# One pool of 2 KB pages, 120 f pairs by seven products, and rounded copies fetched by GpSimd transfers

## The chip, the cores and the metric

The kernel runs on one core of one Trainium2 chip. The metric is the device time of one execution in microseconds (us); the median of three runs stands for the kernel. The engines are TensorE (PE, with PEld for its weight loads), VectorE (DVE), ScalarE (ACT), GpSimd (POOL) and SyncE (SP), which issues the transfers. SBUF is the on-chip memory, PSUM the eight banks that TensorE writes into.

## The reference

Two steps, cut to what matters. The inputs are float32, 4 batches of 6080 tokens with 256 channels; the hidden width f is 2048; w_in and w_out arrive in a 64-bit type.

```python
def _attn_ref(q, k, v, tau):                       # 4 x 6080 x 256 each
    qn = q / (np.linalg.norm(q, axis=1, keepdims=True) + 1e-06)
    kn = k / (np.linalg.norm(k, axis=1, keepdims=True) + 1e-06)
    s = kn.transpose(0, 2, 1) @ qn / tau           # 256 x 256 for each batch, the gram
    a = softmax(s)                                 # over the last axis
    return v @ a
def _moe_ref(x, w_in, w_out):                      # x: 24320 x 256
    h = x @ w_in                                   # 256 -> 2048
    g = np.where(h >= 1, h, np.where(h <= -1, 0.0, (h + 1) ** 2 / 4.0))
    return (g @ w_out).astype(np.float32)          # 2048 -> 256
```

## The kernel before

**What is computed where.** For each batch b, `gram_chunk` and `softmax` make the attention matrix, and `make_W7` (or `make_W` in the first batch) multiplies it into w_in, so that h = v @ (a @ w_in) is one product. The tokens of a batch are cut into six blocks k: five of 2 x 512 tokens and a last one of 2 x 480 (`pairs`). The hidden width is cut into eight pieces i of 256 ("f pairs", two halves of 128). One group is one (b, k, i); there are 4 x 6 x 8 = 192. `h_ops` makes the h of a group as a 2 x 2 block product in seven instead of eight block products (`strassen`); `sat_ops`, `square_ops` and `max_ops` apply the activation; `operand` makes from each of the four blocks the operand of the second product.

**Three matmuls for one product.** The matmuls take the float32r type. To keep precision, every operand is split into a high part (a copy rounded to float32r: a cast on ACT, or on DVE) and a low part (source minus high part: a subtraction on DVE, or on POOL). `mm3` (line 594) issues high x high, high x low and low x high. So one block product is three matmuls of 128 x 128 weights by 512 or 480 columns.

**The second product.** `o_ops` multiplies the four blocks of a group with w_out into four PSUM banks O00, O01, O10, O11, summed over i. Written directly that is eight block products (24 matmuls) for a group. For the first `SPLIT[b][k]` values of i, `strassen_o` does seven instead: four direct ones, and three in a chain into bank O01, on sums of the blocks. These cost other work: `combos` makes three sums of the activations in four subtractions (POOL or DVE); the sums have to be split into high and low parts in turn; and when the last i of them is done, the banks are copied or added out into SBUF between the three stages of the chain (`copy` on ACT and line 1071 on DVE). The summed weights lie in `wsum`; those of the fourth i are parked in DRAM and fetched again for each batch (`guest`). The table SPLIT adds up to 80 of the 192 groups.

**Gram and value copies.** `gram_chunk` loads 256 tokens of k and q (512 KB, on the SP queue), rounds them on ACT (line 603, 54 times), subtracts on DVE (line 604) and has 12 matmuls of 256 columns on PE. `make_V` loads the values of a block, makes four differences of them (line 879, POOL or DVE) and splits seven operands into high (line 885 on ACT or 887 on DVE) and low (line 889 on DVE).

**What sets the order.** The kernel is a list of operations, each with an engine (some with a second one in `other`), its reads and writes, and a due time. `Order.run` goes through them with a table of costs and picks for each engine the next one; what comes out is the fixed instruction order of every engine. Due times come from the tables DUES and LATE. Buffers come from pools of one size and one purpose each (`g`, `u`, `c`, `q`, `m5`, `h22`, `kqs`); who gets a free one is decided in the same run. Each engine works through its own queue strictly in order, so a late instruction holds everything behind it. `tie` makes a POOL operation wait for a given DVE operation, so that both don't use SBUF at once.

## Time and profile before

| what | value |
|---|---|
| median of 3 runs | 2113.44 us (2112.09 to 2113.67) |
| span of the profiled execution | 2112.1 us |
| PE busy | 2102.0 us, 9634 records |
| DVE busy | 1925.6 us, 91% of the span |
| ACT busy | 1786.5 us, 85% |
| POOL busy | 665.0 us, 31% |
| DMA | 374 MB, mean 177 GB/s |

The profiled execution's own time is its span, 2112.1 us, which is the lower end of the three runs and 1.3 us under their median. The granted TensorE clock is 1.000 for the whole span. A busy share counts the time from an instruction's start to its end, where instructions of one engine may overlap; the pitch (from one start to the next) is shorter than the duration. For PE the ends are modelled, so its busy share says little, and the pitch of its matmuls is the better measure.

### The profile page before, as it was taken

How to read it: one execution, taken by the hardware profiler on the slowest of the kernel's cores; microseconds unless marked ns; L12 is line 12 of the kernel's file. 1: busy time of each engine (PE TensorE's matmuls, PEld its weight loads, DVE VectorE, ACT ScalarE, POOL GpSimd, SP SyncE). 2: the span in 40 equal slices, each digit the busy share in tenths (PEclk: the TensorE clock that was granted, in tenths of full speed). 3: DMA queues.
4: the chain of work that ended last, by engine and by line, in shares of the span. 5: the costliest groups of instructions: out<-in, count | busy, mean ns of one | idle time of the engine just before them, and what ended most of it. 6: DMA issues, size and time to landing. Idle time of an engine off the chain costs nothing.

```text
span 2112.1 us, 29105 instructions
## 1 busy us (share of the span) xinstructions
PE 2102.0 (100%) x9634; PEld 1752.6 (83%) x9634; DVE 1925.6 (91%) x3024; ACT 1786.5 (85%) x3255; POOL 665.0 (31%) x621
## 2 busy tenths in 40 slices
PE   9999999999999999999999999999999999999999
PEld 7878888788888888888888888888888888888887
DVE  8998898989899999999889899999997989989987
ACT  6698898988898888889889888888888878888886
POOL 0133133333232333314323233332332333342331
PEclk9999999999999999999999999999999999999999
DMA  9854466544756535544475555454456442432431
GB/s 385 310 204 168 153 230 205 170 162 146 253 173 221 193 139 186 181 163 155 161 243 199 188 185 181 152 197 158 146 196 212 154 145 90 142 127 93 139 112 68
DMA packets 124568, 374.16 MB, mean 177 GB/s; under 512 B 17280, under 2 KB 48896, under 8 KB 121856
## 3 DMA queue, kind: packets, MB, share of 16 engines
q1 hardware_dynamic: 124416, 372.29, 50.4%
q8 instruction: 76, 1.25, 0.2%
q14 instruction: 76, 0.62, 0.1%
HBM read 300.94 MB, written 71.31 MB: 176 GB/s over the span
## 4 chain that ended last, share of the span: by engine, by line
PE 93%; DVE 2%; DMA 2%; ACT 1%; issue 0%; SPq 0%; POOL 0%; ACTq 0%; DVEq 0%; POOLq 0%
PE bank L594 93%; DMA kq<-kq 1%; DMA raw_mem<-w_out 1%; PE bank L1141 1%; DVE u_mem L943 0%; DMA raw_mem<-kq 0%; DVE x L963 0%; DVE u_mem L488 0%; DVE u_mem L491 0%; ACT u_mem L938 0%; DVE w_mem L836 0%; ACT y_mem L1156 0%; ACT u_mem L934 0%; DVE x L1064 0%; DVE u_mem L486 0%
## 5 line engine op out<-in xcount | busy, mean ns | idle before, releaser
L594 PE MATMUL bank<-v,w_mem 128*128 128x512 f32 (+1 forms) x3216 | 832.6, 389 | 2.3 <-ACT bank L774 1.0
L594 PEld LDWEIGHTS bank<-v,w_mem 128*128 128x128 f32 x3216 | 598.8, 188 | 129.0 <-DVE bank L777 4.2
L594 PE MATMUL bank<-x,wout 128*128 128x512 f32 (+1 forms) x2670 | 681.0, 388 | 0.0
L594 PEld LDWEIGHTS bank<-x,wout 128*128 128x128 f32 x2670 | 500.0, 188 | 100.1 <-POOL x L963 0.5
L934 ACT ACTIVATE u_mem<-bank 128x512 f32<-128x512 f32 (+1 forms) x576 | 339.7, 593 | 168.9 <-PE bank L594 163.0
L938 ACT ACTIVATE u_mem<-u_mem 128x512 f32<-128x512 f32 (+1 forms) x768 | 471.6, 628 | 6.6
L943 DVE TENSOR_TENSOR u_mem<-bank,u_mem 128x512 f32<-128x512 f32 (+1 forms) x576 | 385.5, 676 | 70.5 <-ACT u_mem L938 68.9
L963 POOL TENSOR_TENSOR x<-u_mem,x 128x512 fp32r<-128x512 f32 (+1 forms) x162 | 210.0, 1299 | 421.5 <-DVE x L960 104.9
L963 DVE TENSOR_TENSOR x<-u_mem,x 128x512 fp32r<-128x512 f32 (+1 forms) x410 | 308.9, 767 | 3.4 <-ACT x L958 2.6
L958 ACT CAST x<-u_mem 128x512 fp32r<-128x512 f32 (+1 forms) x414 | 247.6, 615 | 34.8 <-DVE u_mem L943 20.9
L594 PE MATMUL bank<-g,wout 128*128 128x512 f32 (+1 forms) x882 | 232.8, 388 | 0.0
L594 PE MATMUL bank<-x,w_mem 128*128 128x512 f32 (+1 forms) x816 | 224.2, 389 | 0.3 <-DVE u_mem L943 0.3
L594 PEld LDWEIGHTS bank<-g,wout 128*128 128x128 f32 x882 | 165.2, 188 | 33.4 <-POOL g L963 0.4
L943 DVE TENSOR_TENSOR u_mem<-mh_mem,u_mem 128x512 f32<-128x512 f32 (+1 forms) x192 | 147.9, 770 | 37.2 <-ACT u_mem L938 36.9
L594 PEld LDWEIGHTS bank<-x,w_mem 128*128 128x128 f32 x816 | 151.9, 188 | 32.6 <-DVE u_mem L943 1.1
L1005 POOL TENSOR_TENSOR q<-u_mem 128x512 f32<-128x512 f32 (+1 forms) x81 | 104.2, 1286 | 193.9 <-DVE u_mem L943 66.6
L934 ACT ACTIVATE u_mem<-mh_mem 128x512 f32<-128x512 f32 (+1 forms) x192 | 120.0, 625 | 27.0 <-DVE mh_mem L781 24.9
L777 DVE TENSOR_TENSOR bank<-bank,mh_mem 128x512 f32<-128x512 f32 (+1 forms) x198 | 135.5, 684 | 5.5 <-PE bank L594 3.4
L781 DVE TENSOR_TENSOR mh_mem<-bank,mh_mem 128x512 f32<-128x512 f32 (+1 forms) x198 | 133.6, 675 | 1.5 <-PE bank L594 0.8
L594 PE MATMUL bank<-x,wsum 128*128 128x512 f32 (+1 forms) x492 | 131.6, 388 | 0.2 <-DVE c L1071 0.2
L879 POOL TENSOR_TENSOR raw_mem<-raw_mem 128x512 f32<-128x512 f32 (+1 forms) x56 | 71.9, 1284 | 166.8 <-DVE x L963 63.6
L963 POOL TENSOR_TENSOR g<-u_mem,g 128x512 fp32r<-128x512 f32 (+1 forms) x55 | 72.2, 1314 | 165.1 <-DVE g L960 38.8
(143 smaller groups left out, 2689.8 us busy)
## 6 DMA issues: line engine op xcount, KB each, us to landing
w_mem<-w_d SPq DMA_DIRECT2D x160, 896.0 KB, 4.6
raw_mem<-kqT SPq DMA_DIRECT2D x60, 512.0 KB, 5.4
w_d<-w_mem SPq DMA_DIRECT2D x32, 896.0 KB, 4.2
raw_mem<-kq SPq DMA_DIRECT2D x51, 512.0 KB, 5.5
kq<-kq SPq DMA_DIRECT2D x20, 1024.0 KB, 9.7
raw_mem<-vT SPq DMA_DIRECT2D x40, 512.0 KB, 6.2
q<-wop_d SPq DMA_DIRECT2D x30, 512.0 KB, 5.7
outT<-c SPq DMA_DIRECT2D x51, 256.0 KB, 2.1
```

The lines of the kernel that those rows point to most:

```text
L594: nc.tensor.matmul(out, lhsT=lhs(a), rhs=rhs(c), start=start and m == 0, stop=stop and m == 2, skip_group_check=skip)
L777: op("DVE", dve_us(n), lambda: nc.vector.tensor_tensor(out=bb.ap[:, :n], in0=z.ap[:, :n], in1=m5.ap[:, :n], op=ALU.add), r=[z, m5], w=[bb] ...
L781: op("DVE", dve_us(n), lambda: nc.vector.tensor_tensor(out=h22.ap[:, :n], in0=z.ap[:, :n], in1=m5.ap[:, :n], op=ALU.add), r=[z, m5], w=[h2 ...
L879: return lambda: e.tensor_tensor(out=part(o), in0=part(a), in1=part(c), op=ALU.subtract)
L934: op("ACT", act_us(n), lambda: nc.scalar.activation(half_of(u, x, n), h.ap[:, :n], IDENTITY_SAT240, scale=240.0), r=[h], w=[u.parts[x]], t ...
L938: op("ACT", act_us(n * (1 + (x is None))), lambda: nc.scalar.activation(part_of(u, x, n), part_of(u, x, n), AF.Square, bias=0.5, scale=1.0 ...
L943: op("DVE", dve_us(n), lambda: nc.vector.tensor_tensor(out=us(), in0=h.ap[:, :n], in1=us(), op=ALU.max), r=[h], w=[u.parts[x]], h=[u], due ...
L958: op("ACT", act_us(cols), lambda x=x: nc.scalar.copy(part(0, x), part_of(u, x, n)), r=of(u.parts, x), w=of(t.parts, x), h=[u, t], due=due, ...
L963: return lambda: e.tensor_tensor(out=part(1, x), in0=part_of(u, x, n), in1=f32(part(0, x)), op=ALU.subtract)
L1005: return lambda: e.tensor_tensor(out=half_of(out, o, n), in0=half_of(a, x, n), in1=half_of(c_, y, n), op=ALU.subtract)
L1141: nc.tensor.matmul(g.ap[:, it * C:(it + 1) * C], lhsT=rb.ap[:p, k0:k0 + P], rhs=rb.ap[:p, t * 512 + C:t * 512 + 2 * C], start=(r0 == 0 and ...
```

## The change

**Seven products for 120 groups.** SPLIT grows to a sum of 120, up to 6 of the 8 values of i. The chain of a block is cut into segments: ENDS says after which i the banks are brought out (for 5: after 3 and 5; for 6: after 3 and 6). A segment that is not the last brings O01 out four times and starts anew; the results are added up in SBUF pages (`into`: the first time an ACT copy, later a DVE addition). All sums of weights have a place in SBUF (`wsum`), made by `late_sums` shortly before they are first used; `guest` is gone.

**One pool of 2 KB pages.** The pools `g`, `u`, `c`, `kqs`, `m5`, `h22` and most of `q` become one pool `pg` of 40 pages of 512 columns each. High and low part of an operand are two pages, each taken and freed by itself. Loads of 512 KB that went into one buffer become two of 256 KB where their target is two pages (`make_W7`, `make_w_in`, `sums_w_in`).

**Rounding transfers.** `cast_load` lets POOL issue a DMA from DRAM whose target is float32r: it brings the rounded high part directly. `gram_chunk` fetches each chunk a second time that way (2 transfers of 256 KB for each of 54 chunks) and drops the ACT cast; its subtraction becomes two of 512 columns. `make_V` fetches the high parts of V_11, V_21 and V_22 that way in all but the first block (69 transfers).

**Engines.** A cast of `operand` may go to ACT, DVE or POOL, a low part to DVE or POOL. Two of the four activations of a group that is not among the 120 are written back into their PSUM bank (KEPT) and split from there by ACT and DVE. The cost table of the planner changes, and in place of due times ORDER gives every operation a rank of its own (a table of numbers, of which no row is shown).

```diff
-SPLIT = ((2, 2, 3, 4, 4, 3), (2, 4, 4, 4, 3, 3), (2, 4, 4, 4, 3, 3), (2, 4, 4, 4, 4, 4))
+SPLIT = ((2, 2, 3, 4, 5, 5), (5, 5, 6, 6, 6, 5), (5, 5, 6, 6, 6, 5), (5, 5, 6, 6, 6, 5))
+ENDS = {1: (1,), 2: (2,), 3: (3,), 4: (4,), 5: (3, 5), 6: (3, 6), 7: (2, 5, 7), 8: (2, 5, 8)}
+KEPT = (("00", "01"),) * 8
+RANK = [n + int(x) for n, x in enumerate(ORDER.split())]
...
-        "u": Pool([u_mem[:, i * 1024:(i + 1) * 1024] for i in range(5)]),
-        "c": Pool([c_first, *[sb(f"c{i}", [TB]) for i in range(1, CN)], y_mem[:, :TB], y_mem[:, TB:]]),
...
+    pools["pg"] = Pool(pages, only={k: rows_(k in "txy", *x) for k, x in FLEX.items()})
...
+    def cast_load(b, src, dst, due, size, gates=(), h=()):
+
+        return op("POOL", DMA, lambda: nc.gpsimd.dma_start(out=dst(), in_=src()), w=[b], h=h, due=due, gates=gates, size=size,
+                  slack=LAND + CAST)
...
-        op("ACT", act_us(1024), lambda: nc.scalar.copy(flat(sb_.ap[:p, 0]), rb.ap[:p]), r=[rb], w=[sb_], due=due)
...
+        for t in range(RT):
+            cast_load(x[t][0], lambda t=t: chunk()[:, t], lambda t=t: x[t][0].ap[:p], due - 12, p * 2048, gates)
+            op("DVE", dve_us(TB), lambda t=t: nc.vector.tensor_tensor(
+                out=x[t][1].ap[:p], in0=rb.ap[:p, t * TB:(t + 1) * TB], in1=f32(x[t][0].ap[:p]), op=ALU.subtract),
+               r=[rb, x[t][0]], w=[x[t][1]], due=due + LATE["gr"][0])
...
+            if (b, k) > (0, 0) and x in (V_11, V_21, V_22):
+                c0 = t0 + src[0] * n
+                cast_load(vs[x], lambda: vT[b, src[1] * P:(src[1] + 1) * P, c0:c0 + n], lambda: vs[x].ap[:, 0, :n],
+                          due + d - 16, 128 * n * 4, gates)
...
+        op("ACT", act_us(n), cast("ACT"), r=[src], w=[t[0]], due=hi, other=() if kept else [
+            ("DVE", dve1_us(n), cast("DVE"), LATE["alt"][later[0]]), ("POOL", pool1_us(n), cast("POOL"), LATE["alt"][later[1]])])
+        op("DVE", dve_us(n), low(nc.vector), r=[src, t[0]], w=[t[1]], due=lo, other=() if kept else [
+            ("POOL", pool_us(n), low(nc.gpsimd), LATE["alt"][later[2]])])
...
-        if i < SPLIT[b][k] - 1:
+        if i < ends[at] - 1:
             return
...
+        def into(x, src, due):
+            if x not in r:
+                r[x] = page("r")
+                op("ACT", act_us(n), lambda: nc.scalar.copy(r[x].ap[:, :n], src.ap[:, :n]), r=[src], w=[r[x]], due=due)
+            else:
+                op("DVE", dve_us(n), lambda: nc.vector.tensor_tensor(
+                    out=r[x].ap[:, :n], in0=src.ap[:, :n], in1=r[x].ap[:, :n], op=ALU.add), r=[src, r[x]], w=[r[x]], due=due)
...
+        into((0, 0), z, early[0])
+        if last:
+            into((1, 0), o(1, 1), early[0])
+        stage(0, lambda j: s_(j, 1))
+        into((1, 0), z, early[1])
+        stage(1, lambda j: s_(j, 2))
+        into((1, 1), z, early[2])
+        stage(2, lambda j: w_(j, 1, 1))
+        if not last:
+            into((0, 1), z, early[3])
```

**What it does to the queues.** Counted over the whole program, PE has 120 matmuls fewer (99 of 512 columns, 21 of 480) and is otherwise the same in kind and number. DVE has 3177 instructions instead of 3026, ACT 3302 instead of 3177, POOL 968 instead of 626, of which 177 are transfers, SP 750 instead of 693.

On PE, the chain of the first block of the second batch (b = 1, k = 0), before. bank_112 is O01; two f pairs stand in the chain. `x_818`, `g_95` and `x_754` are operands, `v_...` and `x_1141` values for the h product.

```order
L594 MATMUL bank_112<-x_818,wsum 128x512 x3
L594 MATMUL bank_116<-v_100,w_mem 128x512 x3
L594 MATMUL bank_110<-x_1141,w_mem 128x512 x3
L594 MATMUL bank_112<-g_95,wsum 128x512 x6
L594 MATMUL bank_113<-x_823,wout 128x512 x3
L594 MATMUL bank_114<-x_823,wout 128x512 x3
L594 MATMUL bank_111<-x_818,wout 128x512 x3
L594 MATMUL bank_116<-x_1141,w_mem 128x512 x3
L594 MATMUL bank_109<-v_99,w_mem 128x512 x3
L594 MATMUL bank_112<-x_754,wout 128x512 x3
```

And the same block after, in its first segment, where bank_107 is O01 and high and low part of an operand are two pages (so one product takes three rows).

```order
L948 MATMUL bank_107<-p_485_5416,wsum 128x512
L948 MATMUL bank_107<-p_487_5433,wsum 128x512
L948 MATMUL bank_107<-p_485_5416,wsum 128x512
L948 MATMUL bank_107<-p_500_5581,wsum 128x512
L948 MATMUL bank_107<-x_905,wsum 128x512
L948 MATMUL bank_107<-p_500_5581,wsum 128x512
L948 MATMUL bank_107<-x_870,wsum 128x512
L948 MATMUL bank_107<-p_507_5628,wsum 128x512
L948 MATMUL bank_107<-x_870,wsum 128x512
L948 MATMUL bank_110<-v_95,w_mem 128x512 x3
L948 MATMUL bank_104<-x_1054,w_mem 128x512 x3
L948 MATMUL bank_107<-x_870,wout 128x512
```

The second stage of the chain has three products here instead of two, and this block has a second such segment of two pairs, of which there was none before.

On DVE, in the same block, before, around its only addition out of O01 (L1071).

```order
L963 TENSOR_TENSOR x_823<-u_mem,x_823 128x512
L1064 TENSOR_TENSOR x_818<-q_50_4967,x_818 128x512
L777 TENSOR_TENSOR bank_110<-bank_116,mh_mem 128x512
L1064 TENSOR_TENSOR g_95<-q_50_4967,g_95 128x512
L943 TENSOR_TENSOR u_mem<-mh_mem,u_mem 128x512
L1071 TENSOR_TENSOR c_63<-bank_112,c_63 128x512
L781 TENSOR_TENSOR mh_mem<-bank_116,mh_mem 128x512
```

After, at the second segment of the block; L1405 is the addition of `into`, L1359 a difference of `combos`, L1314 a low part, L959 a low part of a gram chunk, L1252 one of the values.

```order
L1359 TENSOR_TENSOR mh_mem<-p_523_5799,p_540_5965 128x512
L1314 TENSOR_TENSOR p_545_5992<-p_540_5965,p_541_5977 128x512
L1135 TENSOR_TENSOR u_mem<-bank_111,u_mem 128x512
L1314 TENSOR_TENSOR x_870<-bank_105,p_543_5984 128x512
L1405 TENSOR_TENSOR y_mem<-bank_107,y_mem 128x512
L1252 TENSOR_TENSOR v_102<-raw_mem,v_102 128x512
L959 TENSOR_TENSOR x_905<-raw_mem,p_520_5774 128x512
L959 TENSOR_TENSOR x_905<-raw_mem,x_881 128x512
L1131 TENSOR_TENSOR bank_105<-bank_110,y_mem 128x512
L1301 TENSOR_TENSOR u_mem<-bank_111,u_mem 128x512
L1301 TENSOR_TENSOR p_548_6011<-u_mem,p_548_6011 128x512
L1405 TENSOR_TENSOR p_524_5801<-bank_107,p_524_5801 128x512
```

DVE has more differences and additions here, and the low parts of a gram chunk now stand behind two transfers of POOL instead of an ACT cast.

On POOL, in the second batch, around the third block, before: low parts (L963) and differences (L1005) alone.

```order
L1005 TENSOR_TENSOR u_mem<-u_mem 128x512
L1005 TENSOR_TENSOR q_56_6395<-u_mem 128x512
L963 TENSOR_TENSOR g_95<-u_mem,g_95 128x512
L1005 TENSOR_TENSOR q_57_6483<-u_mem 128x512
L1005 TENSOR_TENSOR u_mem<-u_mem 128x512
L963 TENSOR_TENSOR g_95<-u_mem,g_95 128x512
```

After: transfers of gram copies (`kq`) and value copies (`vT`), a cast (L1311), differences (L1359) and low parts (L1314).

```order
L825 DMA p_581_6417<-kq 128x512
L825 DMA x_870<-kq 128x512
L1359 TENSOR_TENSOR p_584_6431<-mh_mem,y_mem 128x512
L1359 TENSOR_TENSOR u_mem<-mh_mem,y_mem 128x512
L825 DMA p_594_6488<-kq 128x512
L825 DMA x_905<-kq 128x512
L825 DMA v_100<-vT 128x512
L825 DMA v_99<-vT 128x512
L825 DMA v_101<-vT 128x512
L1311 CAST p_596_6521<-c_63 128x512
L1314 TENSOR_TENSOR x_881<-c_63,p_596_6521 128x512
L1359 TENSOR_TENSOR u_mem<-mh_mem,y_mem 128x512
```

The transfers stand in one queue with the arithmetic; what is behind a transfer that waits for its page waits too.

## Rows read from the trace of the kernel before

**Rows 1.** The page: span, busy time by engine, shares of the chain.

```profile
span 2112.1 us, 29105 instructions
...
PE 2102.0 (100%) x9634; PEld 1752.6 (83%) x9634; DVE 1925.6 (91%) x3024; ACT 1786.5 (85%) x3255; POOL 665.0 (31%) x621
...
PE 93%; DVE 2%; DMA 2%; ACT 1%; issue 0%; SPq 0%; POOL 0%; ACTq 0%; DVEq 0%; POOLq 0%
```

**Rows 2.** Chain of work in order of time: start us, us, what; longest piece.

```profile
1141.85 925.20 PE bank L594 x4224
```

**Rows 3.** Waits of PE: us in total, times, longest; after the start.

```profile
PE bank L594 <- DVE u_mem L943: 1.5, 3, 0.8
...
PE bank L594 <- ACT bank L774: 1.0, 2, 0.7
PE bank L594 <- DVE bank L777: 0.5, 1, 0.5
```

**Rows 4.** Windows of 100 us: busy time, clock, DMA share.

```profile
0.00:100.00 100.00, 97.09 (x459) 83.02 (x460) 87.62 (x138) 64.00 (x92) 9.20 (x24) 1.00 0.92 361
...
700.00:800.00 100.00, 100.00 (x473) 83.18 (x472) 95.98 (x143) 86.51 (x159) 34.53 (x27) 1.00 0.51 177
800.00:900.00 100.00, 100.00 (x475) 83.41 (x474) 94.29 (x142) 88.47 (x163) 38.99 (x30) 1.00 0.49 177
900.00:1000.00 100.00, 100.00 (x475) 83.70 (x474) 96.26 (x148) 88.21 (x161) 32.31 (x26) 1.00 0.45 159
```

**Rows 5.** Timeline of PE: start us, us, what; columns 512 and 480.

```profile
1200.94 2.88 PE L594 MATMUL bank<-x,wout 128*128 128x512 f32 x12
1203.66 0.84 PE L594 MATMUL bank<-v,w_mem 128*128 128x512 f32 x3
...
2099.09 6.01 PE L594 MATMUL bank<-x,wout 128*128 128x480 f32 x27
2104.93 1.46 PE L594 MATMUL bank<-g,wout 128*128 128x480 f32 x6
```

**Rows 6.** DVE groups by form: busy us, mean ns, idle before.

```profile
L963 DVE TENSOR_TENSOR x<-u_mem,x 128x512 fp32r<-128x512 f32 x336 | 258.7, 782 | 1.9 <-ACT x L958 1.6
...
L1005 DVE TENSOR_TENSOR q<-u_mem 128x512 f32<-128x512 f32 x66 | 45.3, 686 | 1.0
...
L960 DVE CAST x<-u_mem 128x512 fp32r<-128x512 f32 x127 | 56.3, 452 | 4.6 <-PE bank L594 2.6
...
L1005 DVE TENSOR_TENSOR c<-u_mem,q 128x512 f32<-128x512 f32 x15 | 15.2, 1016 | 1.0 <-POOL q L1005 1.0
...
L1071 DVE TENSOR_TENSOR c<-bank,c 128x512 f32<-128x512 f32 x12 | 8.1, 679 | 0.2 <-PE bank L594 0.2
```

**Rows 7.** Timeline of DVE: three low parts in a row.

```profile
861.40 1.89 DVE L963 TENSOR_TENSOR x<-u_mem,x 128x512 fp32r<-128x512 f32 x3
```

**Rows 8.** ACT groups by form.

```profile
L603 ACT CAST kqs<-raw_mem 128x1024 fp32r<-128x1024 f32 x51 | 53.5, 1049 | 9.9 <-PE bank L594 8.7 <-DMA raw_mem<-kq 1.2
...
L885 ACT CAST v<-raw_mem 128x512 fp32r<-128x512 f32 x87 | 53.3, 618 | 9.4 <-DVE raw_mem L879 7.5 <-PE bank L594 0.6 <-POOL raw_mem L879 0.4
...
L1061 ACT CAST x<-q 128x512 fp32r<-128x512 f32 x68 | 41.5, 624 | 0.5 <-DVE q L1005 0.3
```

**Rows 9.** POOL groups by form.

```profile
L963 POOL TENSOR_TENSOR x<-u_mem,x 128x512 fp32r<-128x512 f32 x138 | 180.5, 1311 | 325.2 <-DVE x L960 87.4 <-DVE x L963 67.3 <-ACT x L958 34.7
...
L1005 POOL TENSOR_TENSOR q<-u_mem 128x512 f32<-128x512 f32 x68 | 88.2, 1298 | 162.3 <-DVE u_mem L943 45.9 <-DVE u_mem L1005 39.1 <-DVE x L1064 24.5
```

**Rows 10.** Waits: DVE for ACT, POOL for DVE, the longest of each.

```profile
DVE u_mem L943 <- ACT u_mem L938: 105.7, 131, 3.2
POOL x L963 <- DVE x L960: 104.9, 20, 13.5
```

**Rows 11.** Transfers: queue; issues with KB each and us to landing.

```profile
q1 hardware_dynamic: 124416, 372.29, 50.4%
...
raw_mem<-kq SPq DMA_DIRECT2D x51, 512.0 KB, 5.5
...
outT<-c SPq DMA_DIRECT2D x51, 256.0 KB, 2.1
```

More of the change, by code (lines that the diff above doesn't have):

```diff
@@ L283 @@
 GRAM_END = -1
-KQS_J = (2, 3)
+CAST = 1.0
+AT_ONCE = 4
+DMA = "dma", 0, 0.0
 W_AT = (3, 1)
@@ L891, in halves, with round_ @@
                r=[parts_of(src)], w=[vs[x]], h=[raws[src[0]]], due=due + d + 1)
+        def round_(x, src, d):
+            op("ACT", act_us(n), lambda: nc.scalar.copy(vs[x].ap[:, 0, :n], part(src)), r=[parts_of(src)], w=[vs[x]],
+               h=[raws[src[0]]], due=due + d, gates=gates,
+               other=[("DVE", dve1_us(n), lambda: nc.vector.tensor_copy(vs[x].ap[:, 0, :n], part(src)), LATE["alt"][5]),
+                      ("POOL", pool1_us(n), lambda: nc.gpsimd.tensor_copy(vs[x].ap[:, 0, :n], part(src)), LATE["alt"][6])]
+               if (b, k) > (0, 1) else ())
         z = spread
@@ L951, in operand @@
[L951 to L966 removed]
+        return 0.005 + 3 * (0.0133 + n * 0.000418)
@@ new lines, in operand, with cast, low @@
+    def operand(src, n, hi, lo, later, kind="t"):
+        t = page(kind), page(kind)
+        kept = src.pool.bank
+        def cast(e):
+            f = nc.scalar.copy if e == "ACT" else {"DVE": nc.vector, "POOL": nc.gpsimd}[e].tensor_copy
+            return lambda: f(t[0].ap[:, :n], src.ap[:, :n])
+        def low(e):
+            return lambda: e.tensor_tensor(out=t[1].ap[:, :n], in0=src.ap[:, :n], in1=f32(t[0].ap)[:, :n], op=ALU.subtract)
+        op("ACT", act_us(n), cast("ACT"), r=[src], w=[t[0]], due=hi, other=() if kept else [
+            ("DVE", dve1_us(n), cast("DVE"), LATE["alt"][later[0]]), ("POOL", pool1_us(n), cast("POOL"), LATE["alt"][later[1]])])
+        op("DVE", dve_us(n), low(nc.vector), r=[src, t[0]], w=[t[1]], due=lo, other=() if kept else [
+            ("POOL", pool_us(n), low(nc.gpsimd), LATE["alt"][later[2]])])
@@ L1029, in strassen_o @@
                     o_buf[b, k, y, ct] = buf(f"O{y}{ct}")
+            sums[b, k] = {}
         o = lambda y, ct: o_buf[b, k, y, ct]
[L1032 to L1038 removed]
@@ new lines, in stage @@
+        def stage(m, weights):
+            for j in range(first, ends[at]):
+                q = DUES[row(k, j)]
+                c = sums[b, k, j][m]
+                t = operand(c, n, d + q["hi"][m], d + q["lo"][m], (2, 8, 9), "x")
+                mm(z, weights(j), t, False, d + q["chain"][m])
+        into((0, 0), z, early[0])
[4 more added lines that the diff above has]
+        stage(1, lambda j: s_(j, 2))
@@ L1186, in channel_attention_moe @@
         else:
-            (make_w_in if kind == "in" else make_w_out)(i, at(due), [kq_ops[gate_]], kq_ops[gate_].due + 0.1)
+            (make_w_in if kind == "in" else make_w_out)(i, at(due), [kq_ops[gate_]], kq_ops[gate_].due["SP"] + 0.1)
     NG = len(groups)
+    i_ = lambda g: groups[g][2]
+    sum_at = {}
+    for j in range(SPLIT[0][0], most):
+        sum_at[next((b, k, j) for b in range(B) for k in range(KP) if SPLIT[b][k] > j)] = True
     for g, (b, k, i) in enumerate(groups):
@@ L1200, in channel_attention_moe @@
                 make_W7((g + q) // (KP * FP), sb_, d + LATE["W7"], gate(g - 2))
-        if i == 0 and b not in guests and SPLIT[b][k] > homed:
-            guest(b, d + LATE["guest"], gate(g - 3))
+        if g + SUM_AHEAD < NG and sum_at.get(groups[g + SUM_AHEAD]):
+            late_sums(i_(g + SUM_AHEAD), d + LATE["sums"], gate(g - 2))
         h_ops(g)
```

467 lines of the change are left out of this document (234 added, 233 removed), and 318 rows, old and new, of tables (DUES, ORDER).

## The prediction

> **What bounds the kernel now.** I read the page first [rows 1]: the span is 2112.1 us, PE is busy for all of it, and PE holds 93% of the chain that ended last. The chain in order of time says the same more plainly: from 1141.85 on, 4224 matmuls follow one another for 925.20 us without anything else in between [rows 2]. Since the ends of matmuls are modelled, a busy PE could still be a slow one, so the second thing to read is its pitch, in stretches of one kind: twelve matmuls of 512 columns take 1203.66 - 1200.94 = 2.72 us, 226.7 ns each, and 27 of 480 columns take 2104.93 - 2099.09 = 5.84 us, 216.3 ns each [rows 5]. The third is what PE waits for: after the start it is 1.5 us for the activation's maximum on DVE, 1.0 for a copy on ACT, 0.5 for an addition on DVE [rows 3]. So the time is the number of matmuls times their pitch, plus a start. The fourth view is how much room the others have: DVE 1925.6 us, ACT 1786.5, POOL 665.0 [rows 1], and from 700 to 1000 us DVE is 94.29 to 96.26% busy while PE still shows 100.00 [rows 4]. DVE is the engine to watch.
>
> **The change on PE.** Each group that goes from eight to seven products saves one product, three matmuls. SPLIT grows from 80 to 120, so 40 products or 120 matmuls go; 7 of the 40 groups lie in the last block (13 to 20 there), so 21 matmuls have 480 columns and 99 have 512. 99 x 226.7 ns + 21 x 216.3 ns = 22.4 + 4.5 = 27.0 us. All of it lies on the path, as nothing else sets the end. The page's span less this is 2085.1 us. The runs' median is 1.3 us above the profiled span, which makes 2086.4. The clock is granted at 1.00, the 2.4 GHz level, in every window read [rows 4]; I keep it.
>
> **The change on DVE.** Counts are from the two instruction orders, durations from [rows 6]. Differences of the seven-product sums: 480 instead of 320, of which DVE takes 313 instead of 138; 175 x 0.686 = +120 us. Additions out of PSUM: 84 instead of 24 because blocks have two segments now, and 92 instead of 72 at the end of a block; 80 x 0.679 = +54. Low parts: 1128 instead of 1008, POOL takes 100 more of them, so DVE has 20 more, +16 at 0.782; but 144 now read a PSUM bank, and DVE instructions that do so take 0.679 where those with both sources in SBUF take 0.782, -15. Casts of operands: 101 instead of 266, -165 x 0.452 = -75. Values: 24 casts and 6 differences fewer, about -15. Gram low parts: 108 of 512 columns for 54 of twice that, and the weight sums; +5 to +15, say +10. Sum +95 us, 2021 us, 96.9% of 2085. Both ends: three low parts in a row take 1.89 us [rows 7], so with one duration of 0.68 the pitch is 0.60, and at that pitch the 255 new differences and additions cost 153 instead of 174; at the 1.016 of a difference that meets POOL [rows 6] the 175 would cost 58 more. DVE lands between 2000 and 2079 us.
>
> **The change on ACT and POOL.** ACT gets 230 operand casts (972 for 742) at 0.624, +144; it loses the 54 gram casts at 1.049, -57, and 60 value casts at 0.618, -37 [rows 8]; copies out of PSUM even out. 1786.5 + 50 = 1836, 88%: covered by PE with some 250 us to spare. POOL gets 100 low parts at 1.311, +131, loses 15 differences at 1.298, -20, and gains 6 value differences and 4 weight sums, +13 [rows 9]. Its 70 casts are in no row: between DVE's 0.452 and POOL's own subtraction of 1.311 they cost 32 to 92 us. Issuing a transfer is in no row either: from nothing to one subtraction, 0 to 232 us for 177. I take the middle of both, since a cast reads one source instead of two and a transfer moves no data through POOL: 665 + 124 + 60 + 115 = 964 us, 46% (bounds 821 to 1113, 39 to 53%). POOL's waits are in the main for DVE [rows 10], it has the room. For the price of an issue the Trainium skill has about 1 us of emission by GpSimd for a transfer (DMA: Bandwidth & Descriptors, section Latency and other measured facts); by that the 177 would be an estimated 177 us, inside the bounds, and no row here shows it.
>
> **Transfers.** 44 MB more (177 x 250 KB) on 372 MB: 50.4% of the engines' time becomes 56% [rows 11]. In time, a 256 KB copy should land between the 2.1 us of the 256 KB stores and the 5.5 of the 512 KB loads [rows 11]; the gram copy stands beside the SP load of the same data, which it needs too, so I cost it at nothing. What hides it is the distance in POOL's queue; without that cover, every low part behind it on DVE is late, and PE's gram product after it.
>
> **Start and end.** The start keeps its loads; the sums of two of the first w_out pieces move out of it. PE's idle time in the first 100 us is 2.9 us [rows 4]; I take no change, bounds -3 to +3. The last groups are the same.
>
> **What is added to PE's waiting.** Before, waits of this kind come to 3.0 us [rows 3] with DVE idle for 186 us of the span. After, DVE has about 64 us idle (6 to 85 by the bounds). I double the 3.0 and get 3 more: 2086.4 + 3 = 2089. Why no more: in the window of 96.26% PE lost nothing [rows 4], and the pitch of 0.60 against durations of 0.68 to 0.78 says that a busy share of 96% still leaves DVE able to go some 10% faster when work is waiting.
>
> **Rivals.**
> A. *DVE becomes the bound, and part of the gain is lost.* No window read has DVE above 96.26%, and the forecast needs 96.9% on average. Much of its idle time is a wait for ACT's square in the same chain of operations (105.7 us [rows 10]), which the change does not remove. If DVE can be kept no denser than 96.26%, the time is 2021 / 0.9626 = 2100, and with the 1.3 us 2101; if no denser than 95.5%, the mean of the three windows, 2116 + 1 = 2118, which is slower. Against it stands the pitch argument above. It takes from the gain where gram work and six-pair blocks meet, in the second and third batch. I put its time at 2096 to 2112.
> B. *The rounding transfers hold the queues, and the kernel is slower.* They are 177 waits for a landing that DVE's low part stands behind, and POOL has to be free to issue each in time; a queue in order passes a delay on to everything behind. The place is DVE's L959 and L1252, and the price is 177 times whatever of the lateness reaches PE: the gain of 27 us is gone at 0.15 us for each. DVE's mean cast of 0.452 us is one measure of a possible delay; if half of that reaches PE it is 177 x 0.226 = 40 us, 2086.4 + 40 = 2126. For it: these waits fall on an engine that has little room. Against it: POOL is idle for half the span, and a page is taken well ahead. The Trainium skill speaks against such transfers beside DVE work (SBUF — State Buffer, section Who interferes with whom): while DVE runs a copy or cast in a two-port mode, GpSimd cannot write its descriptors, so a transfer issued from there waits. DVE keeps 119 such casts, about 54 us or 2.6% of the span by the row of 0.452, so few transfers would meet one; no row here shows a transfer from POOL.
> C. *The new order also clears the old waits.* The span is 10.1 us longer than PE's busy time [rows 1], 2.9 of it in the first 100 us [rows 4]. If the start runs better by those 2.9 us and nothing is added to PE's waiting, 2083; without any idle time 2076.
> That the change does not do what it says is not among them: the 120 matmuls are counted in the order.
>
> **How the numbers follow.** Forecast, PE stays fed: 2089, range 2083 to 2096, 0.56. A: 2096 to 2109 with 0.18, and 0.07 up to 2118. B: 0.13, around 2126. C: 0.06. Some 0.2%, 4.2 us, is what a measurement of this kernel can tell from no change. Faster than 2109.2: 0.56 + 0.18 + 0.06 = 0.80; within 0.2%: 0.07; slower: 0.13. The range leaves out the better part of C and the slower cases: 2080 to 2112.
>
> **What would show it.** PE with 9514 records (120 fewer) at the same 226.7 ns of pitch; DVE near 2021 us and 97%; ACT at 88%; POOL near 960 us with the transfers' issue as the unknown; the waits of PE still single microseconds, for DVE and ACT. For A, windows in the second and third batch in which PE falls under 100% while DVE stands at 97 or more. For B, waits of DVE or PE for transfers into pages, or of POOL's arithmetic behind its transfers, of over 20 us in sum. I am wrong if PE's waits come to more than 10 us, or if its pitch changes with the pages.

## The result, and the profile after

| | before | after |
|---|---|---|
| median | 2113.18 us (2112.09 to 2113.67, 4 runs) | 2126.39 us (2123.76 to 2127.31, 4 runs) |
| span of the profiled execution | 2112.1 us | 2124.7 us |
| ratio of the runs | | 1.0059, 95% interval 1.0045 to 1.0073 |

The changed kernel is slower by 13 us, 0.6%. The forecast was 2089, with a range of 2080 to 2112. TensorE lost its 120 matmuls as counted; the time is 40 us above the sum of 2086.4 that the prediction made without any added waiting.

The page of the changed kernel, the lines that answer to [rows 1]:

```profile
span 2124.7 us, 30300 instructions
...
PE 2099.7 (99%) x9514; PEld 1720.8 (81%) x9514; DVE 1999.5 (94%) x3175; ACT 1833.8 (86%) x3380; POOL 917.1 (43%) x963
...
PE 67%; DVE 18%; ACT 6%; DMA 4%; issue 3%; POOL 1%; SPq 0%; DVEq 0%; POOLq 0%; ACTq 0%
```

PE has the 9514 records that were announced. The third line has the news: PE held 93% of the chain that ended last and now holds 67%; DVE has 18% of it. PE still shows 99% busy, and that is the trap of this page: a matmul's record lasts some 390 ns while the next one starts 227 ns later, so a record covers up to 160 ns of a wait. The pitch itself is as before. Timeline of PE in the changed kernel (start us, us, what), groups of three matmuls of 512 columns and nine of 480, for [rows 5]:

```profile
1212.22 0.85 PE L948 MATMUL bank<-x,wout 128*128 128x512 f32 x3
1212.91 0.84 PE L948 MATMUL bank<-p,wout 128*128 128x512 f32 x3
1213.59 0.84 PE L948 MATMUL bank<-x,w_mem 128*128 128x512 f32 x3
1214.27 0.39 PE L948 MATMUL bank<-p,wout 128*128 128x512 f32 x1
...
2090.09 2.11 PE L948 MATMUL bank<-p,wsum 128*128 128x480 f32 x9
2092.04 1.46 PE L948 MATMUL bank<-v,w_mem 128*128 128x480 f32 x6
```

Nine matmuls from 1212.22 to 1214.27 are 228 ns each, nine of 480 columns 217. So the work on PE is what the prediction says, and everything above it is waiting. The place to read that is the table of waits of the weight loads (PEld), which stand ahead of their matmuls, not that of the matmuls, whose long records hide short waits: those of the steady line add up to 15.5 us in 32 waits there. Waits of PEld in the changed kernel (us in total, times, longest):

```profile
PEld bank L948 <- DVE bank L1131: 15.3, 45, 1.2
PEld bank L948 <- ACT bank L1128: 14.4, 33, 1.3
PEld bank L948 <- DVE p L1314: 7.0, 13, 0.9
```

and the same view of the kernel before, which the prediction did not read:

```profile
PEld bank L594 <- DVE u_mem L943: 5.3, 15, 1.2
PEld bank L594 <- DVE bank L777: 4.2, 14, 0.9
...
PEld bank L594 <- ACT bank L774: 2.8, 6, 1.1
```

All rows of this view for the steady line (L594 before, L948 after) add up to 19.9 us in 60 waits before and 73.1 us in 184 after. Of the 73.1, 52.7 are for DVE, 18.4 for ACT, 1.2 for POOL and 0.4 for a transfer. (Not all of such a wait reaches a matmul: 53 us more of them stand beside 40 us of time.) L1131, L1128 and L1135 are operations on banks and sums inside `strassen`, L1314 the low parts.

Windows of 100 us of the changed kernel (PE, PEld, DVE, ACT, POOL busy with records, clock, DMA share, GB/s), for [rows 4]:

```profile
600.00:700.00 100.00, 97.06 (x443) 77.45 (x442) 97.16 (x151) 89.23 (x165) 51.55 (x63) 1.00 0.69 222
700.00:800.00 100.00, 99.94 (x476) 82.64 (x475) 96.68 (x152) 89.12 (x165) 51.15 (x51) 1.00 0.64 225
800.00:900.00 100.00, 99.06 (x466) 81.40 (x465) 96.92 (x151) 87.54 (x165) 52.86 (x54) 1.00 0.65 216
900.00:1000.00 100.00, 98.15 (x456) 79.64 (x455) 95.97 (x151) 88.04 (x165) 49.79 (x50) 1.00 0.62 202
1100.00:1200.00 100.00, 96.04 (x430) 76.68 (x429) 93.52 (x149) 90.17 (x165) 42.79 (x62) 1.00 0.64 208
1400.00:1500.00 100.00, 99.78 (x467) 81.49 (x466) 98.95 (x153) 88.10 (x164) 48.96 (x49) 1.00 0.63 214
```

Two of the windows before:

```profile
600.00:700.00 100.00, 99.87 (x468) 83.20 (x467) 94.00 (x146) 86.78 (x156) 32.06 (x37) 1.00 0.58 198
1100.00:1200.00 100.00, 99.85 (x465) 83.39 (x464) 93.32 (x143) 91.58 (x164) 33.01 (x43) 1.00 0.60 203
```

PE fell under 100% nearly everywhere, and behind the first 100 us most at 600 and 1100 us, where batches 1 and 2 start. The chain in order of time (start us, us, what) shows such a place:

```profile
1140.18 0.69 DVE y_mem L1359
1140.86 0.60 DVE x L1314
1141.47 0.60 DVE u_mem L1359
1142.07 0.63 DVE x L1314
1142.74 1.59 PE bank L948 x5
```

DVE goes from one instruction to the next without a gap, at a pitch of 0.60 to 0.68, and PE starts when DVE's low part has just ended.

### The profile page after: what moved, and what is told of

Its sections match the earlier page's. It is cut to its first block, busy times and chain, and to the rows that moved or that the text cites. A ratio compares the mean times of both kernels' runs of the same rounds, so it can differ in the third digit from the quotient of the medians.

```text
span 2124.7 us, 30300 instructions
## 1 busy us (share of the span) xinstructions
PE 2099.7 (99%) x9514; PEld 1720.8 (81%) x9514; DVE 1999.5 (94%) x3175; ACT 1833.8 (86%) x3380; POOL 917.1 (43%) x963
## 3 DMA queue, kind: packets, MB, share of 16 engines
q1 hardware_dynamic: 128528, 369.67, 49.9%
q8 instruction: 75, 1.23, 0.2%
## 4 chain that ended last, share of the span: by engine, by line
PE 67%; DVE 18%; ACT 6%; DMA 4%; issue 3%; POOL 1%; SPq 0%; DVEq 0%; POOLq 0%; ACTq 0%
PE bank L948 65%; DVE p L1314 2%; DVE x L1314 2%; DVE bank L1131 1%; DMA kq<-kq 1%; DVE p L1359 1%; PE bank L1487 1%; DVE p L1301 1%; DVE u_mem L1301 1%; DVE v L1252 1%; DMA raw_mem<-kq 1%; ACT p L1311 1%; ACT x L1311 1%; DMA x<-kq 1%; DMA raw_mem<-kqT 1%
## 5 line engine op out<-in xcount | busy, mean ns | idle before, releaser
L948 PE MATMUL bank<-v,w_mem 128*128 128x512 f32 (+1 forms) x3288 | 869.6, 392 | 8.7 <-ACT bank L1128 2.7
L948 PEld LDWEIGHTS bank<-v,w_mem 128*128 128x128 f32 x3288 | 606.7, 188 | 156.2 <-DVE bank L1131 11.3
L948 PE MATMUL bank<-p,wout 128*128 128x512 f32 (+1 forms) x1692 | 540.4, 389 | 1.4 <-DVE p L1314 1.3
L948 PE MATMUL bank<-x,wout 128*128 128x512 f32 (+1 forms) x1449 | 473.6, 389 | 1.0 <-DVE x L1314 0.7
L948 PEld LDWEIGHTS bank<-p,wout 128*128 128x128 f32 x1692 | 316.6, 188 | 69.5 <-DVE p L1314 3.3
L948 PEld LDWEIGHTS bank<-x,wout 128*128 128x128 f32 x1449 | 271.2, 188 | 58.2 <-DVE x L1314 2.2
L948 PE MATMUL bank<-x,w_mem 128*128 128x512 f32 (+1 forms) x744 | 208.8, 391 | 2.4 <-ACT bank L1128 1.6
L948 PE MATMUL bank<-p,wsum 128*128 128x512 f32 (+1 forms) x600 | 193.6, 391 | 1.2 <-DVE p L1314 1.0
L948 PE MATMUL bank<-x,wsum 128*128 128x512 f32 (+1 forms) x507 | 167.6, 391 | 0.8 <-DVE x L1314 0.6
L948 PEld LDWEIGHTS bank<-x,w_mem 128*128 128x128 f32 x744 | 137.4, 188 | 35.4 <-ACT bank L1128 4.0
L1296 ACT ACTIVATE p<-p 128x512 f32<-128x512 f32 (+1 forms) x247 | 154.4, 630 | 2.1
L1296 ACT ACTIVATE u_mem<-u_mem 128x512 f32<-128x512 f32 (+1 forms) x228 | 142.6, 630 | 2.8
L948 PEld LDWEIGHTS bank<-p,wsum 128*128 128x128 f32 x600 | 111.8, 188 | 27.0 <-DVE p L1314 3.4
L1292 ACT ACTIVATE p<-bank 128x512 f32<-128x512 f32 (+1 forms) x195 | 115.2, 592 | 13.3 <-PE bank L948 12.6
L1292 ACT ACTIVATE u_mem<-bank 128x512 f32<-128x512 f32 (+1 forms) x168 | 99.2, 592 | 27.8 <-PE bank L948 27.2
L1128 ACT COPY bank<-bank 128x512 f32<-128x512 f32 (+1 forms) x198 | 115.5, 583 | 4.3 <-PE bank L948 1.8
L948 PEld LDWEIGHTS bank<-x,wsum 128*128 128x128 f32 x507 | 94.9, 188 | 22.7 <-DVE x L1314 2.0
L1252 DVE TENSOR_TENSOR v<-raw_mem,v 128x512 fp32r<-128x512 f32 (+1 forms) x137 | 107.0, 786 | 6.0 <-DMA raw_mem<-vT 3.2
L1311 ACT CAST p<-p 128x512 fp32r<-128x512 f32 (+1 forms) x153 | 94.1, 616 | 17.0 <-DVE p L1301 7.9
```

The source lines that it names most:

```text
L948: nc.tensor.matmul(out, lhsT=lhs(a), rhs=rhs(c), start=start and m == 0, stop=stop and m == 2, skip_group_check=skip)
L1128: op("ACT", act_us(n), lambda: nc.scalar.copy(a.ap[:, :n], z.ap[:, :n]), r=[z], w=[a], due=early[1])
L1252: op("DVE", dve_us(n), lambda: nc.vector.tensor_tensor(out=vs[x].ap[:, 1, :n], in0=part(src), in1=f32(vs[x].ap[:, 0, :n]), op=ALU.subtract ...
L1292: op("ACT", act_us(n), lambda: nc.scalar.activation(u.ap[:, :n], h.ap[:, :n], IDENTITY_SAT240, scale=240.0), r=[h], w=[u], table="sat", du ...
L1296: op("ACT", act_us(n), lambda: nc.scalar.activation(u.ap[:, :n], u.ap[:, :n], AF.Square, bias=0.5, scale=1.0 / 480.0), r=[u], w=[u], due=due)
L1311: return lambda: f(t[0].ap[:, :n], src.ap[:, :n])
```

## The experiments

Three theories stood at the start. **Theory 1**: DVE's queue is full, and PE and ACT wait for it. **Theory 2**: transfers are late or hold queues (the rounding ones move 46 MB). **Theory 3**: POOL's longer work keeps DVE off a shared way to SBUF. The kernels called "cheaper" keep every queue's order as it is in the changed kernel and replace operations of two inputs by copies of one (e7 and e12 also cut squares short), which leaves arithmetic out; what moves the time there is the duration alone. (In their traces PE, DVE, ACT and POOL write the same results in the same order as in the changed kernel.) The ratios are to runs of the kernel before that were taken beside them (medians of 2113.2 to 2114.1 us).

| run | median us | ratio to before, interval | DVE | ACT | POOL busy |
|---|---|---|---|---|---|
| after | 2126.39 | 1.0059, 1.0045 to 1.0073 | 1999.5 | 1833.8 | 917.1 |
| e1, DVE cheaper | 2110.80 | 0.9984, 0.9974 to 0.9993 | 1936.0 | 1829.2 | 917.5 |
| e2, half of the W loads | 2117.15 | 1.0019, 1.0010 to 1.0028 | 1998.5 | 1833.0 | 917.6 |
| e3, POOL cheaper | 2110.14 | 0.9981, 0.9972 to 0.9991 | 1926.3 | 1829.4 | 592.9 |
| e5, DVE and POOL cheaper | 2107.18 | 0.9968, 0.9957 to 0.9979 | 1767.7 | 1824.6 | 597.4 |
| e7, and ACT | 2097.35 | 0.9916, 0.9900 to 0.9933 | 1763.4 | 1623.2 | 597.1 |
| e12, and half of the W loads | 2089.64 | 0.9879, 0.9863 to 0.9896 | 1763.1 | 1624.2 | 599.7 |
| e6, *before* with DVE dearer | 2175.33 | 1.0294, 1.0277 to 1.0311 | 2004.4 | 1796.5 | 676.8 |

**e1: DVE cheaper.**

```diff
         def low(e):
+            if kind == "x" and e is nc.vector:
+                return lambda: e.tensor_copy(t[1].ap[:, :n], src.ap[:, :n])
             return lambda: e.tensor_tensor(... op=ALU.subtract)
```

> The changed kernel with its order of instructions kept on every engine; of the low halves of the combined f pages (operand kind x), the 255 that VectorE makes are a copy of the page (one input) in place of the subtraction (two inputs). That leaves the low-half arithmetic out, so the time is that of the same program with some 255 x 0.26 us = 66 us less on VectorE, and nothing else changed. Theory 1 (VectorE's queue is full, TensorE and ScalarE wait for it): VectorE falls from 1999 to about 1935 us, back to the share it had before the change, and of the 42 us that TensorE loses behind the first 300 us some 30 go: 2090 to 2102 us. Theory 2 (the rounding transfers are late or hold queues): the waits for landings stay, 2118 to 2127 us. Theory 3 (GpSimd's longer work keeps VectorE off the shared port): 2112 to 2122 us.

63.5 us less on DVE gave 15.6 us back. That is theory 1's direction and about half of its size, so its range is missed. Theory 3's range is missed by 1.2 us, and POOL is unchanged here; theory 2's is missed by 7.2. A quarter of a us for each us of DVE also says that DVE's work does not simply bound the kernel.

**e2: half of each W load.**

```diff
-        load(w, lambda: w_dram[b][i], lambda: w.ap..., due, ...)
+        load(w, lambda: w_dram[b][i][:, :WSZ // 2], lambda: w.ap[:, 0]..., due, ...)
```

> The changed kernel with its order kept; each of the 160 loads of a W page moves only the first half (448 KB in place of 896 KB), so the low half of W is left out and stays stale. That takes 73 MB out of the transfers, more than the 46 MB that the rounding transfers brought. Theory 1 (VectorE's queue is full): nothing to gain, 2120 to 2127 us. Theory 2 (transfers land late because the change made more of them): landings fall to or under those of before and 20 to 30 us come back, 2095 to 2108 us. Theory 3 (GpSimd and the port): 2120 to 2127 us.

Its transfers (queue, MB, share; KB each, us to landing):

```profile
q1 hardware_dynamic: 128528, 296.27, 41.6%
...
w_mem<-w_d SPq DMA_DIRECT2D x160, 448.0 KB, 3.4
...
raw_mem<-kq SPq DMA_DIRECT2D x51, 512.0 KB, 5.4
```

9 us come back, between the two theories. The gram's raw load lands after 5.4 us, as before the change (5.5, [rows 11]), in place of 6.7. So landings have a part in the loss, a smaller one. Which landings, the W loads' own or the others that became shorter beside them, is not shown.

**e3: POOL cheaper.**

```diff
         def low(e):
+            if e is nc.gpsimd:
+                return lambda: e.tensor_copy(t[1].ap[:, :n], src.ap[:, :n])
...
             def less(e, out=out, a=a, c=c):
+                if e is nc.gpsimd:
+                    return lambda: e.tensor_copy(out.ap[:, :n], a.ap[:, :n])
```

> The changed kernel with its order kept; on GpSimd alone, the subtractions of the low halves and of the combinations are copies of one input (0.56 us in place of 1.25), so that arithmetic is left out. GpSimd's busy time falls from 917 to about 650 us with the same instructions at the same places. Theory 3 (GpSimd's longer work keeps VectorE off the shared port and its results come late): 2095 to 2110 us. Theory 1 (VectorE's own work fills it): 2115 to 2127 us, since VectorE has as much to do as before. Theory 2 (transfers): 2118 to 2127 us.

16 us come back, 2110.14 at the upper end of theory 3's range; but look where. One group of DVE by form (busy us, mean ns, idle before), in the changed kernel and then in e3, the same instructions with the same operands (L1316 in e3 is L1314, two lines further down):

```profile
L1314 DVE TENSOR_TENSOR x<-p,p 128x512 fp32r<-128x512 f32 x44 | 33.3, 759 | 1.4 <-ACT p L1311 1.4
```

```profile
L1316 DVE TENSOR_TENSOR x<-p,p 128x512 fp32r<-128x512 f32 x44 | 30.1, 685 | 1.9 <-ACT p L1311 1.8
```

With POOL's operations shorter, DVE's own busy time falls by 73 us without one DVE instruction changed. DVE gains 73 us here and 63.5 in e1, and the time falls by 16 in both: so DVE's time is the likely lever of e3 too. It is not the only thing that moved: POOL's results also come earlier, and the waits for them fall from 14.3 to 5.3 us on ACT and from 1.9 to 0.9 on DVE. How the 16 us divide between the two is not shown. The lengthening of DVE's instructions by POOL was there before the change: then, the same kind of DVE instruction had 782 ns on average [rows 6], more than after.

**e4: roundings by engines again.**

```diff
-            cast_load(x[t][0], ...)
+            op("ACT", act_us(TB), ..., other=[("DVE", ...), ("POOL", ...)])
...
-            if (b, k) > (0, 0) and x in (V_11, V_21, V_22):
+            if False:
```

> The changed kernel without its rounding transfers: the 177 roundings of gram and value pages are casts again, on ScalarE unless the planner takes VectorE or GpSimd; the 120 products and the single page pool stay, and the planner lays out the order anew with the same ranks. Theory 1 (the vector engines are full): 177 casts of 0.34 to 0.56 us go to full engines, TensorE waits for most of them: 2145 to 2190 us. Theory 2 (the rounding transfers are what was lost): 2095 to 2115 us. Theory 3 (GpSimd and the port): 2115 to 2140 us, since GpSimd loses 98 us of issue but VectorE gains casts.

2185.99 us, DVE 2057.8 and ACT 1873.5 us busy. This is in theory 1's range (ratio 1.0338), but it proves less than it seems: the planner laid the order out anew with ranks that were made for other operations, and how much of the 60 us is casts and how much is a poor order can't be told apart. What the rounding transfers are worth by themselves stays open.

**e5: every low part cheaper, on DVE and POOL.** The two edits of e1 and e3 together, with e1's for every kind.

> The changed kernel with its order kept; every subtraction for a low half of an f page, on VectorE and on GpSimd, and GpSimd's subtractions for the combined pages are copies of one input, so that arithmetic is left out: some 811 x 0.26 = 210 us less on VectorE and 325 us less on GpSimd. TensorE's work and the order of every queue are those of the changed kernel, so this is what the order costs when the vector engines are no limit. Theory 1 (VectorE's fill is the cause): VectorE near 1720 us; beyond the two cheaper kernels before it (2110 each) only little more comes back, since what is left are waits that the order itself has at the starts of batches 1 to 3: 2095 to 2104 us. Theory 1b (VectorE's fill is the whole of it, the order has no waits of its own): 2082 to 2092 us. Theory 2 (transfers): 2108 to 2120 us.

232 us less on DVE than in the changed kernel give 19 us, hardly more than the first 63 did, and 2107.18 misses all three ranges. PEld's waits for DVE in the steady line fell from 52.7 to 19.1 us, those for ACT stayed (18.4 and 17.6). So cheaper work on DVE and POOL gives back 19 of the 40 us, and behind it stands something else. Of what PE's matmuls still wait for in e5, this is the longest (us in total, times, longest):

```profile
PE bank L948 <- ACT bank L1128: 5.9, 8, 2.1
```

**e6: the old kernel with DVE dearer.** The counterpart: 308 casts of the kernel before get a second input and keep their values.

```diff
-  lambda x=x: nc.vector.tensor_copy(part(0, x), part_of(u, x, n))
+  lambda x=x: nc.vector.tensor_tensor(out=part(0, x), in0=part_of(u, x, n), in1=part_of(u, x, n), op=ALU.max)
```

> The kernel before with its order kept on every engine; its 308 casts on VectorE are made by an operation of two inputs (the maximum of the page with itself), which takes some 0.26 us more each and gives the same values: about 80 us more on VectorE (1926 to about 2005 us, what the changed kernel has), with 80 pairs of f pages, no rounding transfers and the old pools. Theory 1 (VectorE's fill is the cause): TensorE's waiting grows as it did in the changed kernel: 2125 to 2155 us. Theory 2 (the transfers or GpSimd's issue of them are the cause) and theory 3 (GpSimd): little happens, 2113 to 2119 us.

Its page, and a window for [rows 4]:

```profile
PE 2140.4 (99%) x9634; PEld 1738.1 (80%) x9634; DVE 2004.4 (92%) x3024; ACT 1796.5 (83%) x3255; POOL 676.8 (31%) x621
...
PE 44%; DVE 43%; ACT 7%; issue 3%; DMA 2%; POOL 1%; SPq 0%; DVEq 0%; ACTq 0%; POOLq 0%
```

```profile
700.00:800.00 100.00, 98.52 (x459) 79.99 (x458) 95.63 (x137) 81.15 (x146) 33.58 (x26) 1.00 0.44 156
```

78.8 us more on DVE cost 61 us (2175.33 against 2114.13 for the kernel before beside it), beyond even theory 1's range, and with no rounding transfer and no new pool. DVE is 92% busy over the whole and 95.63% in this window, less than before (95.98) although its casts are dearer: a busy share does not tell which engine waits for which. The kernel before had PE at 100%, and yet its DVE could not take this work without PE waiting. In e6 the waits of PEld add up to 99.3 us (19.9 before), these two the longest (us in total, times, longest):

```profile
PEld bank L594 <- DVE bank L777: 19.5, 44, 1.2
PEld bank L594 <- DVE x L963: 17.5, 36, 1.2
```

Two things are mixed in the 61 us. The dearer casts stand at the head of a chain (cast, low part, matmul), so each result also comes later; and the order was laid out for the cheaper casts. The changed kernel has as much work on DVE, in an order made for it, and is 49 us faster than e6.

**e7: ACT cheaper too.** e5, and the squares in place on a quarter of their columns.

> The kernel e5 (order of the changed kernel; low halves of f pages and GpSimd's combined pages as copies) with ScalarE made cheaper as well: its 768 squares in place take a quarter of their columns, some 0.32 us less each, about 240 us less on ScalarE; squares of the other columns are left out. The order of every queue stays. Theory 1 (the waits that were left in e5, at the starts of batches 1 to 3, are for vector work too, ScalarE's copies of banks above all): they shrink, and the time comes near TensorE's own work and the start, 2088 to 2098 us. Theory 1c (these waits lie in the order itself, or in transfers, whatever the engines cost): they stay, 2102 to 2108 us.

Another 10 us, as much as theory 1 asks for at the upper end of its range: what e5 had left was in part for ACT. PEld's waits for ACT fell from 17.6 to 10.4 us, those for DVE from 19.1 to 14.4. The squares stand ahead of DVE's maximum in the same chain as well as ahead of the bank copies in ACT's queue; which of the two gave the time is not shown.

**e12: and half of the W loads.** e7 with e2's edit.

> The kernel e7 (order of the changed kernel, all three vector engines made cheaper) with the W loads of e2 (half of each page, the low half of W left out) as well. What e7 left over the sum of the prediction is 2097 - 2086 = 11 us. If that is landings (transfers), it goes: 2087 to 2091 us. If it is waits that lie in the order, it stays: 2094 to 2099 us.

```profile
span 2089.4 us, 30255 instructions
...
PE 2073.0 (99%) x9514; PEld 1732.5 (83%) x9514; DVE 1763.1 (84%) x3175; ACT 1624.2 (78%) x3380; POOL 599.7 (29%) x963
```

2089.64: the same matmuls in the same order, with vector engines and landings out of the way, end 3 us above the prediction's sum of 2086.4, in the range that was given for landings. PEld's waits in the steady line come to 19.1 us, what they were before the change (19.9). This is the account: of the 40 us, 29 come back with cheaper vector engines (e7), some 8 with fewer bytes to land (e2 9.2, e12 against e7 7.7), and 3 are left. It says what PE waits for, not what each part of the change added: e7 leaves DVE with 1763 us and ACT with 1623, well under what they had before the change. The shares depend on which is taken first, as they are not additive: e1 and e3 give 16 each and e5, which holds both, 19.

**e8, e9: other orders.** The same products, transfers and pools as in the changed kernel, with two other tables of ranks. Some operations change their engine by it: DVE has 3217 and 3221 instructions for 3175 and is busy for 2005.4 and 2003.6 us, POOL has 931 and 915 for 963.

```diff
-RANK = [n + int(x) for n, x in enumerate(ORDER.split())]
+RANK = [n + float(x) for n, x in enumerate(ORDER.split())]
```

> The changed kernel with its work unchanged (120 products, 177 rounding transfers, the same pools) and only the table of ranks replaced: the ranks were moved until the order still comes out well when a few landings come up to some us late and each operation a few ns longer than the planner assumes. TensorE's work is the same, VectorE's nearly so (42 more operations, some 25 us more by the planner's durations; GpSimd some 45 us less). Theory 1 (the vector engines are full and the order has no room for anything late): a large part of the small waits goes, those at the starts of batches 1 to 3 stay at some 13 us, since they are in the new order as well: 2102 to 2114 us. Theory 1b (VectorE's amount of work alone decides, whatever the order): 2122 to 2135 us. Theory 2 (transfers): 2118 to 2128 us.

> A second table of ranks, found in the same way from another start, to see whether what the first one shows is a property of such orders or of one of them. Theory 1: within 5 us of the first, 2102 to 2116 us. Theory 1b: 2122 to 2135 us. Theory 2: 2118 to 2128 us.

2120.14 us (ratio 1.0035, 1.0021 to 1.0049) and 2118.00 (1.0022, 1.0013 to 1.0031): 6 and 8 us better than the changed kernel. Theory 1's ranges are missed, theory 1b's by 2 and 4 us; both times lie in theory 2's range, but no transfer was changed here, and DVE has some 5 us more to do, so they are no evidence for it. The order is worth some 6 to 8 us; neither version beats the kernel before.

**e10, e11: where.** What e7 makes cheaper, made cheaper in one column block k of batches 1 to 3 alone.

```diff
     def h_ops(g):
         b, k, i = groups[g]
+        relief[0] = b > 0 and k == 0      # e11: k == 3
```

> The changed kernel with its order kept; what e7 makes cheaper (low halves and GpSimd's combined pages as copies, squares on a quarter of their columns) is made cheaper in the first column block of batches 1 to 3 alone, 3 of the 24 blocks, and that arithmetic is left out there. The change raised the products of these blocks from 2 groups to 5, beside the set-up of the batch. Theory F (the loss lies where the first block's five groups meet the set-up): of the 29 us that e7 gives back, far more than 3/24 comes from here: 2108 to 2117 us. Theory U (the vector engines are too full everywhere alike): 3/24 of 29 us, 2121 to 2125 us.

> The counterpart: the same operations made cheaper in the fourth column block of batches 1 to 3 (six groups by seven products there, four before), and that arithmetic left out there. Theory F: little, 2122 to 2126 us. Theory U: the same as the first blocks, 2121 to 2125 us.

e10: 2116.37 us (ratio 1.0010, 1.0002 to 1.0019), 10.0 us back for 27.1 us of DVE's time (1972.4; POOL and ACT are cheaper there as well). e11: 2120.22 (1.0030, 1.0019 to 1.0041), 6.2 us for 36.3 us (1963.2). e10 is in theory F's range, e11 is in no range, and neither theory holds for both. The first block is the dearer place of the two, with 0.37 us back for each us of DVE against 0.17 in the fourth, but the fourth gives more than its share of 3.6 us too. The other four blocks were not tried.

## Why the prediction was wrong

- **PE**: right. 120 matmuls fewer, pitch 228 and 217 ns, clock granted at 1.00; e12, which leaves arithmetic out, comes within 3 us of the sum that the 27.0 us went into.
- **DVE**: 1999.5 us for 2021, just under the lower bound (2000). **ACT**: 1833.8 for 1836. **POOL**: 917.1 for 964, in its bounds; the 70 casts took 43.2 us in place of 60, the 177 issues 98.3 in place of 115. By the Trainium skill (DMA: Bandwidth & Descriptors, section Latency and other measured facts) an issue was estimated at about 1 us; the rows below, two of the four groups, have 553 and 564 ns of POOL.
- **Transfers**: 49.9 + 7.6 = 57.5% of the engines' time for 56%. The 256 KB copies were to land between 2.1 and 5.5 us; the two largest groups took 5.5 and 6.3, the upper bound and above (the others 5.1 and 6.7), and the raw load of the gram 6.7 in place of 5.5:

```profile
L825 POOL DMA_DIRECT2D p<-kq x64 | 35.3, 553 | 3.4 <-PE bank L948 1.5 <-DVE p L1314 1.1 <-issue 0.7
L825 POOL DMA_DIRECT2D v<-vT x52 | 29.0, 564 | 0.1
```

```profile
q1 hardware_dynamic: 128528, 369.67, 49.9%
q0 software_dynamic: 25296, 45.82, 7.6%
...
raw_mem<-kq SPq DMA_DIRECT2D x51, 512.0 KB, 6.7
...
p<-kq POOLq DMA_DIRECT2D x59, 256.0 KB, 5.5
...
v<-vT POOLq DMA_DIRECT2D x42, 256.0 KB, 6.3
```

- **What is added to PE's waiting**: this is the step that failed. It put 3 us; the runs have 40 (2126.4 - 2086.4), of which 29 come back when the vector engines are made cheaper. Its own sign, more than 10 us of PE's waits, came in: even the matmuls' table has 15.5. Three things went wrong in it. It doubled 3.0 us read from the matmuls' waits [rows 3], where the weight loads' waits held 19.9: the room was smaller than it looked. It reasoned from an average: "a busy share of 96% still leaves DVE able to go some 10% faster when work is waiting" takes the pitch of DVE instructions in a row for a reserve. DVE did work denser: 151 to 152 instructions in the windows from 700 to 1000 us, where it had 142 to 148, and 98.95% busy from 1400. PE waited all the same, since what counts is whether DVE is on time at each bank. And it had no measurement of how PE answers to DVE's time; e6 gives one for the kernel before with its order fixed, 0.78 us for each us.
- **ACT**, costed at nothing ("covered by PE with some 250 us to spare"): with DVE cheaper already, e7 gets 10 us from it. A spare share over the whole span covered nothing where a bank waited for a copy (L1128: 33 waits of PEld, 14.4 us).
- **Transfers costed at nothing**: e2 and e12 put 8 to 9 us on landings. The cover that the prediction named, the distance in POOL's queue, was there for most of the rounding transfers. What DVE itself waited for shows that SP's loads were later than the rounding transfers (us in total, times, longest):

```profile
DVE v L1252 <- DMA raw_mem<-vT: 3.2, 2, 2.0
DVE p L959 <- DMA raw_mem<-kq: 3.2, 2, 2.3
DVE raw_mem L1240 <- DMA raw_mem<-vT: 1.8, 1, 1.8
DVE p L959 <- DMA x<-kq: 1.5, 2, 1.0
DVE p L959 <- DMA p<-kq: 1.3, 1, 1.3
DVE v L1252 <- DMA v<-vT: 1.0, 2, 0.7
```

- **Rival A** (DVE becomes the bound) comes nearest, but the time lies beyond its prices (2096 to 2112, a tail to 2118). Most of the waits are for DVE, as it says. As a bound it fails: DVE stands at 94% over the whole, less dense than its two cases (96.26 and 95.5%), and e5 takes 232 us off DVE for 19 us. DVE is late at single places and idle at others. Its test, PE under 100% where DVE stands at 97 or more, was half right: from 600 us it holds, from 1100 PE loses most with DVE at 93.52%, from 1400 DVE stands at 98.95% and PE loses little. **Rival B** had the right time, 2126, by luck: its waits were to exceed 20 us, and DVE's waits for rounding transfers (x<-kq, p<-kq, v<-vT above) come to 3.8. The rule that went with it, that DVE's two-port copies hold up GpSimd's descriptors (the Trainium skill, SBUF — State Buffer, section Who interferes with whom), shows next to no cost here: the four groups of issues take 553 to 564 ns on average, and POOL idled 3.7 us ahead of all 177. In e5, where all 811 low parts of DVE are copies, the 177 issues take 99.9 us in place of 98.3.

What stays open: what the rounding transfers are worth alone (e4 mixes them with an order), how the 40 us divide among the parts of the change, whether the vector engines cost PE more by their fill or by the later results of each chain, and how many products would be best. A version with fewer products was not tried, since each needs a table of ranks of its own.

## What to carry to other kernels

Read the waits of the weight loads beside those of the matmuls before calling TensorE saturated: records with modelled ends hid 17 of 20 us here. A product that saves three matmuls (0.68 us at 227 ns) costs ten vector operations (four differences, three casts, three low parts) and two additions out of PSUM here; that pays only where the vector engines are early at the banks. Before making them busier, measure the answer by making an operation dearer in the kernel as it is, as e6 does, and keep in mind that its order was made for the cheaper one. And a change of several parts can be taken apart by durations: the same queues with cheaper operations show in a few runs which engine PE waits for.
